# All steps of a fused window-attention and two-layer kernel in a new order, with q and k of batch 0 loaded ahead of most of V

## The chip, the cores and the metric

The kernel runs on one core of one Trainium2 chip. The metric is the device time of that core in microseconds (us). The kernel before takes 312.04 us, the median of three runs from 312.03 to 312.27.

## What is computed

The reference is attention over a causal window of 64 positions, then two matrix products with `h - tanh(h)` between them.

```python
batch, n_heads, seq, head_dim = (8, 8, 576, 64)
...
scores = scale * np.matmul(q, k.transpose(0, 1, 3, 2))
mask = (rel >= 0) & (rel < window)          # rel = query position - key position
attn = softmax(np.where(mask, scores, -1e9))
x = (attn @ v), heads side by side           # 4608 x 512
h = x @ w_in                                 # 512 x 2048
g = h - np.tanh(h)
return g @ w_out                             # 2048 x 512
```

All inputs and the output are float32; the kernel works in bfloat16 and sums in float32.

## The kernel before

**Tiling.** The sequence of a batch is cut into nine windows of 64 queries; a window needs the 128 keys that end with it. Heads are worked in pairs: pair g of 32 holds heads g % 4 and g % 4 + 4 of batch g // 4. Attention writes its result transposed into chunks of 512 tokens (`x_chunk`); a chunk is the moving operand of the first layer, 16 blocks of 128 hidden columns with four matmuls of 512 columns each, and its `g` is the stationary operand of the second layer, four blocks of 128 tokens with 16 matmuls each. There are nine chunks; chunk 0 needs all of batch 0 but its last window.

**The order is written out by hand.** The kernel turns the framework's scheduling off and plays `PLAN`, a string of 1146 words. A word is a step with its arguments, for instance `Rp.1.0.4`: step Rp, pair 1, group 0, PSUM bank 4. A last letter p, a, v or s names the engine: GpSimd (POOL), ScalarE (ACT), VectorE (DVE), SyncE (SP). Each engine works off its own steps in the order of the words; between engines the framework puts semaphore waits wherever two steps touch the same place. So the place of a word decides what stands behind it on the same engine, and which of two steps that touch one place comes first.

The steps that the text speaks of:

- `lk.g`, `lq.g` (`load`, L92 to L109): k or q of pair g from DRAM. On GpSimd's queue the transfer also converts to bfloat16; on SP's it does not. `LV.b.i` (`load_rows`, L140 to L144): 128 rows of V of batch b for all heads (64 rows for i = 4), into the tile `vw`, 64 values a head with a 65th column beside them. `lv.b.pair.half` (`load_v`) and `lt.b`: V of batch 1, head by head. `wi.i`, `wo.i`: blocks of the weights. All but two of the loads are issued by GpSimd, and its queue takes a further one only when the eighth before it has landed.
- `mv.i` (`pads_v`, L199 to L201): two memsets on VectorE in `vw`, the 65th column to one (L200) and a first block of zeros (L201). `mt`, `mq`: zeros beside k and in q. `i`, `h`, `n`: an identity and two masks, made on GpSimd.
- `Z.b` (`cross_rows`, L146 to L150): two copies on VectorE that put the rows of V that a window shares with its neighbour on the other half of the partitions. For batch 1 these are `za` and `zb`, a pair at a time.
- `U.n` (`warm_up`, L217 to L220): n matmuls of 512 columns on a tile of zeros, whose result nobody reads.
- `ck.g`, `cq.g` (`cast`): reorders k or q in SBUF. `Fp.g`, `Ep.g` (`tr`): transposes on TensorE. `Fc`, `Ec`, `Ea`, `Eb` (`put`): copies of these into `kT`, `qp` or `qT`, of which there are two each, used by even and odd pairs.
- `Rp` (`scores`, L273 to L293), `Rx` (`probs`, the exponentials on ScalarE), `M` (`masking`), `N` (`put_mask`).
- `P.g` (`pv`, L334 to L342), `PP.g` (`pv_pairs`): the product with V; its 65th column gives the sum of each row. `D.g`, `DS.g`, `DH.g.n`, `DR`, `DN`: division by that sum, on VectorE.
- `Xp`, `Xc` (L399 to L415): transposes of the result and copies into the chunk.
- `H.c.m` (`first_layer`, matmuls at L437), `A.c.m` (tanh, L445), `G.c.m` (h - tanh(h), L451), `W.c.s.part` (second layer, L480 and L473), `O.c.s` (copy and store of the output).

TensorE's queue goes without a branch through transposes, scores, products with V and both layers, so any one of them that waits holds all the rest. PSUM has eight banks, addressed by number in the words.

```python
    def load_rows(b, i):
        w, n = vw[b % 2], min(128, S - 128 * i)
        nc.gpsimd.dma_start(out=w[:, 2 * i + 1, :, 0:D] if i < NF else w[64:128, 2 * i, :, 0:D],
                            in_=v[b, :, 128 * i:128 * i + n].rearrange("h p d -> p h d"))
...
    def pads_v(i):
        nc.vector.memset(vw[i][:, :, :, D], 1.0)
        nc.vector.memset(vw[i][0:64, 0], 0.0)
```

Of the kernel before, what the change touches and what calls it, by code (L numbers as in the profile page):

```python
# [15 lines left out]
def kernel(  # L16
# [491 lines left out]
    def subtract(c, m, s=None):
# [14 lines left out]
        H=first_layer, A=tanh, G=subtract, W=yp_mm, O=y_out)  # L523

    def play(script):
# [14 lines left out]
        lq.8.p H.0.2 A.0.1 G.0.0 n lv.1.3.1 Rp.4.2.4 ck.7.v G.0.1 H.0.3 Rx.4.2.4 Rp.5.2.4 wo.0 A.0.3 Rx.5.2.4  # L540
        G.0.3 Fp.7.3 H.0.4 Rp.4.0.4 A.0.2 N G.0.2 H.0.6 Rx.4.0.4 Fc.7.3.a M.5 A.0.4 za.1.0.v G.0.4 H.0.5 A.0.6
        lv.1.3.0 Fp.6.3 Rp.4.1.4 A.0.5 Fc.6.3.a G.0.5 H.0.7 zb.1.0.p Ep.7.3 A.0.7 G.0.6 H.0.8 Ea.7.3.a G.0.7
        cq.6.v A.0.8 H.0.9 Eb.7.3.v G.0.8 za.1.1.p Rx.4.1.4 H.0.10 A.0.9 zb.1.1.p lt.1 M.4 Rp.7.0.4 Ep.6.3
        A.0.10 H.0.11 Eb.6.3.a Rx.7.0.4 G.0.9 wo.2 G.0.10 H.0.12 A.0.11 lq.9.p wo.1 Rp.7.2.4 Rx.7.2.4 H.0.13
        wo.3 Ea.6.3.v G.0.11 A.0.12 cq.8.v lk.9.p Rp.6.1.4 H.0.14 G.0.12 Rx.6.1.4 Ep.8.3 ck.8.v H.0.15 A.0.14
# [95 lines left out]
```

## Time and profile before

| | |
|---|---|
| median of three runs | 312.04 us |
| the profiled execution, its own time | 311.42 us |
| its span, from the first instruction to the last | 309.7 us |
| mean granted TensorE clock | 0.989 of full speed |
| busy: TensorE (PE), VectorE, ScalarE, GpSimd | 301.3, 183.7, 156.2, 103.0 us |
| first matmul of the first layer, H.0.0 | starts at 27.93 us |
| last matmul ends | 306.52 us |
| matmuls of the first layer (L437) and of the second (L480) | 380 ns each in the rows, 216 ns from start to start |
| dummy matmuls (L220) | 27 |

A busy time is a union over an engine's instructions, and matmuls overlap, so their rows last longer than the distance of their starts. "PEclk" is the clock that the chip granted to TensorE. L143 and the like are lines of the kernel file.

### The profile page before, as it was taken

Reading aid. Unit: us, or ns where it says so; the run is one execution under the profiler, and the core shown is the slowest. Engines: PE = TensorE matmul, PEld = TensorE weight load, DVE = VectorE, ACT = ScalarE, POOL = GpSimd, SP = SyncE. Lnnn points to the kernel's source line nnn. Section 1 sums busy time; section 2 is a strip of 40 time slices with the busy share of each in tenths; the row PEclk is TensorE's granted clock in tenths of the full one; section 3 lists DMA queues with packets and bytes.
Section 4 is the critical chain, followed back from the end, with each engine's and each line's share of the span. In section 5 each row is a group of like instructions: output and inputs, shape, how many; then the busy total and the mean of one; then the engine's idle time right before and its main releaser. Section 6 shows DMA issues by size and latency. Waiting matters only on the chain.

```text
span 309.7 us, 6275 instructions
## 1 busy us (share of the span) xinstructions
PE 301.3 (97%) x2522; PEld 159.8 (52%) x2522; DVE 183.7 (59%) x321; ACT 156.2 (50%) x266; POOL 103.0 (33%) x139
## 2 busy tenths in 40 slices
PE   8798999999999999999999999999999999999995
PEld 3456555556555545555555555555554444444443
DVE  3558796758947757767557585836566433353301
ACT  3556878579527644643725445555253333444300
POOL 8996475695195028203942700000000000000000
PEclk9959999999999999999999999999999999999999
DMA  9999999999999969998999998350015000000012
GB/s 151 132 176 199 197 182 187 181 169 141 145 137 162 148 117 151 164 155 125 159 160 177 161 179 117 89 134 35 3 70 110 34 35 34 34 34 36 37 65 102
DMA packets 133436, 37.33 MB, mean 121 GB/s; under 512 B 122016, under 2 KB 127904, under 8 KB 133408
## 3 DMA queue, kind: packets, MB, share of 16 engines
q0 software_dynamic: 91184, 18.06, 75.3%
q1 hardware_dynamic: 42224, 18.88, 31.3%
q8 instruction: 19, 0.31, 0.4%
q14 instruction: 9, 0.07, 0.1%
HBM read 36.70 MB, written 9.44 MB: 149 GB/s over the span
## 4 chain that ended last, share of the span: by engine, by line
PE 89%; DVE 3%; POOL 3%; DMA 2%; issue 1%; ACT 1%; POOLq 0%; ACTq 0%; DVEq 0%
PE ps L480 39%; PE ps L437 38%; PE ps L354 3%; PE ps L310 2%; DMA qall<-in_q_dram 2%; POOL vw L143 1%; PE ps L253 1%; DVE gT L451 1%; PE ps L473 1%; PE ps L292 1%; PE ps L403 1%; DVE qt L90 1%; PE ps L281 1%; POOL kall L108 1%; ACT th L445 1%
## 5 line engine op out<-in xcount | busy, mean ns | idle before, releaser
L451 DVE TENSOR_TENSOR gT<-ps,th 128x512 bf16<-128x512 f32 x144 | 97.7, 687 | 79.6 <-ACT th L445 79.0
L437 PE MATMUL ps<-xT,wi 128*128 128x512 bf16 x576 | 140.4, 380 | 0.5 <-DVE gT L451 0.2
L445 ACT ACTIVATE th<-ps 128x512 f32<-128x512 f32 x144 | 85.2, 598 | 100.0 <-PE ps L437 98.6
L480 PE MATMUL ps<-w_out_sb,gT 128*128 128x512 bf16 x560 | 134.3, 380 | 0.0
L437 PEld LDWEIGHTS <-wi 128*128 128x128 bf16 x576 | 63.0, 114 | 54.7 <-issue 0.9
L480 PEld LDWEIGHTS <-gT 128*128 128x128 bf16 x560 | 53.7, 98 | 60.9
L143 POOL DMA_DIRECT2D vw<-in_v_dram x35 | 30.5, 882 | 16.6 <-DVE q L90 9.0
L159 POOL DMA_DIRECT2D kall<-in_k_dram x25 | 21.6, 877 | 26.0 <-DMA kw<-kall 24.9
L159 POOL DMA_DIRECT2D qall<-in_q_dram x25 | 21.8, 879 | 20.9 <-DMA qw<-qall 17.5
L320 ACT ACTIVATE pt<-ps 128x1024 bf16<-128x1024 f32 (+1 forms) x30 | 23.3, 812 | 6.1 <-PE ps L310 5.9
L88 ACT ACTIVATE ysb<-ps 128x512 f32<-128x512 f32 (+1 forms) x20 | 11.6, 582 | 24.8 <-PE ps L480 19.7
L90 DVE COPY ysb<-ps 128x512 f32<-128x512 f32 (+1 forms) x17 | 11.6, 680 | 20.2 <-PE ps L480 19.5
L329 DVE TENSOR_TENSOR pt<-pt,ps 128x1152 bf16<-128x1152 bf16 x28 | 20.5, 746 | 3.2 <-ACT pt L320 2.8
L324 ACT ACTIVATE pt<-ps 128x384 bf16<-128x384 f32 (+2 forms) x32 | 16.9, 528 | 5.3 <-PE ps L292 3.4
L374 DVE TENSOR_TENSOR xs<-ps,rcp 128x384 bf16<-128x384 f32 x28 | 14.8, 550 | 0.2
L354 PEld LDWEIGHTS <-pt 128*64 128x64 bf16 x504 | 9.1, 111 | 5.1 <-issue 1.6
L354 PE MATMUL ps<-vw,pt 128*64 128x65 bf16 x504 | 10.7, 197 | 0.0
L220 PE MATMUL ps<-warm 128*128 128x512 bf16 x27 | 9.2, 498 | 1.1 <-DVE warm L197 1.1
L88 ACT ACTIVATE kt<-ps 128x576 bf16<-128x576 bf16 x10 | 6.5, 648 | 6.5 <-PE ps L253 3.5
L108 POOL DMA_DIRECT2D kall<-in_k_dram x11 | 7.3, 668 | 3.2 <-DMA wi<-in_moe_w_in_dram 1.8
L130 POOL DMA_DIRECT2D vw<-in_v_dram x8 | 6.7, 843 | 4.6 <-DMA wi<-in_moe_w_in_dram 4.5
L292 PE MATMUL ps<-qt,kt 128*128 128x128 bf16 x72 | 8.0, 219 | 0.0
(76 smaller groups left out, 160.5 us busy)
## 6 DMA issues: line engine op xcount, KB each, us to landing
out_dram<-ysb SPq DMA_DIRECT2D x35, 256.0 KB, 3.5
vw<-in_v_dram POOLq DMA_DIRECT2D x28, 128.0 KB, 8.6
kall<-in_k_dram POOLq DMA_DIRECT2D x20, 128.0 KB, 7.1
qall<-in_q_dram POOLq DMA_DIRECT2D x20, 128.0 KB, 7.0
w_out_sb<-in_moe_w_out_dram POOLq DMA_DIRECT2D x4, 512.0 KB, 10.1
kall<-in_k_dram POOLq DMA_DIRECT2D x11, 144.0 KB, 5.2
qall<-in_q_dram POOLq DMA_DIRECT2D x11, 144.0 KB, 7.2
vw<-in_v_dram POOLq DMA_DIRECT2D x16, 64.0 KB, 7.0
```

What stands on the lines that cost most here:

```text
L88: nc.scalar.activation(o, i, ACT.Copy)
L143: nc.gpsimd.dma_start(out=w[:, 2 * i + 1, :, 0:D] if i < NF else w[64:128, 2 * i, :, 0:D], in_=v[b, :, 128 * i:128 * i + n].rearrange("h p ...
L159: nc.gpsimd.dma_start(out=token_rows(b, n)[0:c, i], in_=(q if n == "q" else k)[b, :, 128 * i:128 * i + c].rearrange("h p d -> p h d"))
L320: nc.scalar.activation(o, sp, ACT.Exp, scale=scale)
L324: nc.scalar.activation(PT[g % NPT][:, js[0]:js[0] + len(js), :].rearrange("p i (h t) -> p i h t", h=2), sp, ACT.Exp, scale=scale)
L329: nc.vector.tensor_tensor(p, p, mask.unsqueeze(1).to_broadcast([128, 2 * NJ, 64]), ALU.mult)
L354: nc.tensor.matmul(ps[r, bank, 65 * i:65 * i + 65], PT[(g + r2) % NPT][:, j, r], vw[b % 2][:, j, p0 + r2 + NP * h, :], start=True, stop=True)
L374: nc.vector.tensor_tensor(xs[b % 2][:, 0:6, p0 + n // 2, :], ov[:, :, 0:D], sums[g][:, n].to_broadcast([128, 6, D]), ALU.mult)
L437: nc.tensor.matmul(hp, w_in_tile(ki, m), chunk_tile(c)[:, n.start // 64:n.stop // 64, ki % 2, 64 * (ki // 2):64 * (ki // 2) + 64], start=( ...
L445: nc.scalar.activation(th[:, n], hp, ACT.Tanh)
L451: nc.vector.tensor_tensor(gT[c][:, m, columns(s)], hp, th, ALU.subtract)
L480: nc.tensor.matmul(yp, gT[c][:, m, s * 128:(s + 1) * 128], w_out_sb[:, m, :], start=n == 1 and i == 0, stop=n == 4 and i == 3)
```

## The change

Two things change. A function `first_layer_part` is added, with a step Hp for it, which no word of the list uses. And the list is replaced: the same 1146 words but for the order, for the engine of some of the copies, and for the banks of many transposes and scores, which lay in bank 2, 3 or 4 and now lie in banks 0 to 7. The numbers of transfers, matmuls and dummy matmuls are the same. Here is the start of both lists, up to the first layer, and the new function; the rest of the list is in a new order as well.

```diff
         hidden[c, m, s] = hp_mm(c, m, s)
 
+    def first_layer_part(c, m, half):
+        n = turn("h", c, m)
+        hp = ps[:, m % 2 if c > 1 else (m + c) % 3, :]
+        for i in range(2):
+            nc.tensor.matmul(hp, w_in_tile(half + 2 * i, m), chunk_tile(c)[:, :, half, 64 * i:64 * i + 64],
+                             start=n == 1 and i == 0, stop=n == 2 and i == 1)
+        hidden[c, m, None] = hp
+
     def tanh(c, m, s=None):
         hidden[c, m, s] = squash(s, hidden[c, m, s])
 
...
@@ PLAN
-        mt.1 mt.0 lk.1.p lq.1.p i u mv.0 LV.0.0 lk.5.p U.1 lk.0.s U.1 lq.0.s lq.3.p U.4 LV.0.3 LV.0.4 h LV.0.1
-        cq.0.a U.13 mq.0 mv.1 U.1.3 ck.1.a cq.1.v mq.1 Fp.1.2 Ep.1.3 LV.0.2 Fc.1.2.a U.2 ck.0.v Fp.0.2 lk.3.p
-        Ec.1.3.v Fc.0.2.v Rp.1.1.4 Ep.0.3 Ec.0.3.v Rx.1.1.4 lq.2.p Rp.1.0.0 lv.1.1.1 lk.2.p lq.5.p Rx.1.0.0 U.4
-        Rp.0.1.4 Rp.0.0.0 ck.5.a lk.4.p Z.0 Rx.0.1.4 Ep.3.3 Rx.0.0.0 Fp.3.2 lv.1.0.0 lk.6.p lq.4.p P.0 Fc.3.2.a
-        Ec.3.3.v lk.7.p D.0 Ep.2.3 Rp.3.1.4 Ec.2.3.a Rp.3.0.0 U.1.2 Rx.3.1.4 Fp.5.3 wi.0 Fp.2.2 cq.5.a Fc.5.3.v
-        P.1 lv.1.1.0 ck.4.v D.1 Rx.3.0.0 Fc.2.2.a Ep.5.3 Rp.2.1.4 Eb.5.3.a lq.7.p lv.1.0.1 wi.1 Rp.2.0.0
-        Rx.2.1.4 P.3 Rx.2.0.0 Ea.5.3.v wi.2 Fp.4.3 lq.6.p P.2 Xp.0.0.1.2 cq.4.v Fc.4.3.a Rp.5.0.4 D.3 DS.2
-        Xp.0.0.0.3 Rx.5.0.4 DH.2.0 Xc.0.0.1.2.a Xc.0.0.0.3.v DH.2.1 Xp.0.1.0.3 Xc.0.1.0.3.a Xp.0.1.1.2 Rp.5.1.4
-        Ep.4.3 Xc.0.1.1.2.v ck.6.v Ea.4.3.v Eb.4.3.v H.0.0 H.0.1 lv.1.2.0 A.0.0 Rx.5.1.4 lk.8.p cq.7.v lv.1.2.1
...
+        lq.0.s lk.0.s u LV.0.2 i lk.1.p ck.1.v cq.0.v mt.1 lq.1.p lq.3.p lk.3.p U.1 U.13 ck.0.a LV.0.3 U.4
+        Fp.0.0 U.4 Fc.0.0.a lq.2.p cq.1.v Fp.1.2 Ep.1.7 U.2 LV.0.0 mt.0 LV.0.1 Fc.1.2.v h Fp.3.6 Ep.3.3 Ec.1.7.a
+        lk.5.p lk.2.p Ep.0.5 LV.0.4 Rp.1.1.4 Rp.1.0.0 lq.5.p Rx.1.1.4 Ec.0.5.a Rx.1.0.0 mv.0 Ec.3.3.v lq.4.p
+        mv.1 Rp.0.1.4 U.1 Ep.2.2 Rp.0.0.0 Rx.0.1.4 Z.0 mq.0 Fc.3.6.a Rx.0.0.0 Rp.3.1.4 Fp.2.3 Rx.3.1.4 Rp.3.0.0
+        cq.5.v Fc.2.3.a lv.1.1.1 Ec.2.2.a P.0 lk.4.p lq.6.p Ep.5.3 Rp.2.1.4 U.1.2 D.0 Rx.3.0.0 wi.0 Rp.2.0.0
+        Rx.2.1.4 P.1 cq.4.v lv.1.1.0 Ep.4.2 mq.1 D.1 Rx.2.0.0 P.2 P.3 DS.2 lq.7.p ck.4.v DH.2.0 D.3 Ea.4.2.a
+        Eb.5.3.a Ea.5.3.a Fp.4.4 Xp.0.0.0.0 Xp.0.0.1.7 n lk.6.p U.1.3 DH.2.1 Xp.0.1.0.3 Xc.0.0.1.7.v Fc.4.4.a
+        wi.1 Eb.4.2.a Rp.4.0.4 Xp.0.1.1.5 ck.5.v Xc.0.1.1.5.v cq.6.v Rp.4.1.6 Xc.0.0.0.0.a Rp.4.2.7 Fp.5.1
+        Xc.0.1.0.3.a Fc.5.1.v H.0.0 Rx.4.0.4 A.0.0 Rx.4.2.7 cq.7.v ck.6.v Ep.6.4 H.0.1 H.0.2 G.0.0 A.0.1
+        Ea.6.4.v A.0.2 Rx.4.1.6 H.0.3 Rp.5.1.7 Rx.5.1.7 A.0.3 G.0.1 lk.7.p Rp.5.2.3 za.1.1.p wi.2 lq.8.p G.0.2
+        Ep.7.6 Rp.5.0.5 lv.1.0.1 Rx.5.2.3 H.0.5 ck.7.v Eb.7.6.v Fp.6.7 N lk.8.p A.0.5 Fp.7.3 G.0.3 H.0.4
+        Ea.7.6.a Rx.5.0.5 Fc.7.3.a H.0.6 Eb.6.4.v wo.2 A.0.4 Fc.6.7.v Rp.6.1.5 Rp.7.2.3 Rp.6.0.6 G.0.5 Rp.7.0.4
+        G.0.4 Rp.7.1.7 H.0.8 A.0.6 lv.1.0.0 lt.1 H.0.7 A.0.8 wo.1 A.0.7 G.0.6 M.4 G.0.8 zb.1.1.p wo.0 Rx.6.1.5
...
```

On GpSimd the loads went lk.1, lq.1, LV.0.0, lk.5, lq.3, LV.0.3, LV.0.4, LV.0.1, LV.0.2, lk.3, lq.2 and so on; they now go LV.0.2, lk.1, lq.1, lq.3, lk.3, LV.0.3, lq.2, LV.0.0, LV.0.1, lk.5, lk.2, LV.0.4, lq.5, lq.4, lv.1.1.1, lk.4, lq.6, wi.0. On SP lk.0 and lq.0 change places. On VectorE mv.0 and mv.1 stood ahead of the first V load of their tile; mv.0 now stands behind the five loads of batch 0, after Fc.1.2 and ahead of Ec.3.3, mv.1 and Z.0, and mv.1 still ahead of lv.1.1.1. On TensorE the transposes and scores of pair 3 and the transposes of pair 2 now come ahead of P.0; they came behind it, but for the transposes of pair 3.

More of the change, by code (lines that the diff above doesn't have):

```diff
@@ L522 @@
         P=pv, D=norm, DS=norm_sums, DH=norm_half, PP=pv_pairs, DR=recip_pairs, DN=norm_pairs, Xp=x_tr, Xc=x_put, Y=x_dma,
-        H=first_layer, A=tanh, G=subtract, W=yp_mm, O=y_out)
+        H=first_layer, Hp=first_layer_part, A=tanh, G=subtract, W=yp_mm, O=y_out)
     def play(script):
@@ L541 @@
[L541 to L545, printed above, removed]
@@ new lines @@
+        G.0.14 DR.4 lv.1.2.1 G.0.15 W.0.0.2 Rp.8.2.3 W.0.0.1 DN.4.2 DN.4.0 lk.9.p Rp.8.1.7 lq.10.p M.7 lk.10.p
+        Rx.8.2.3 W.0.1.1 DN.4.1 W.0.1.2 W.0.0.0 Xp.1.0.0.3 Rp.8.0.4 lr.3.4 lq.11.p G.0.13 Rx.8.1.7 Xp.1.0.1.5
+        LV.2.3 M.6 W.0.1.0 W.0.1.3 cq.9.v lk.11.p W.0.0.3 O.0.1.a W.0.3.1 zb.1.2.v Ep.9.1 O.0.0.a W.0.3.2
+        W.0.3.0 zb.1.3.p za.1.2.v za.1.3.v Xc.1.0.0.3.v Rx.8.0.4 Xc.1.0.1.5.a LV.2.0 PP.6 ck.9.a cq.10.v M.8
+        Ep.10.3 DR.6 LV.2.2 W.0.2.3 W.0.2.2 Ea.10.3.a ck.10.a Eb.9.1.a Ea.9.1.a DN.6.1 Eb.10.3.a LV.2.1 Fp.9.6
@@ new lines @@
+        W.0.2.0 DN.6.2 DN.6.0 Fc.9.6.v Xp.1.1.1.1 W.0.2.1 Xp.1.1.0.3 lr.3.2 Rp.9.1.7 O.0.2.a cq.11.v
+        Xc.1.1.0.3.v Xc.1.1.1.1.v W.0.3.3 Rp.9.2.5 H.1.0 Rx.9.1.7 ck.11.a Rx.9.2.5 LV.2.4 qr.3.0 qr.4.3 A.1.0
+        Ep.11.6 Rp.9.0.4 Eb.11.6.a Fp.11.5 Rx.9.0.4 qr.4.4 Fp.10.3 H.1.1 O.0.3.v qr.3.4 H.1.2 Fc.11.5.a LV.3.3
+        LV.3.1 A.1.1 Fc.10.3.a G.1.0 A.1.2 H.1.3 A.1.3 Z.2 G.1.1 Rp.10.2.7 Rp.10.0.4 H.1.4 Rx.10.2.7 A.1.4 G.1.2
+        G.1.3 Ea.11.6.a H.1.5 M.9 G.1.4 H.1.6 A.1.5 Rx.10.0.4 A.1.6 H.1.7 G.1.5 A.1.7 PP.8 lr.4.4 lr.3.0 lr.3.3
@@ new lines @@
+        H.1.8 G.1.6 Rp.11.2.4 A.1.8 G.1.7 Rp.11.0.3 H.1.10 A.1.10 DR.8 H.1.9 LV.3.4 DN.8.0 lr.3.1 qr.3.3 DN.8.2
+        G.1.8 DN.8.1 qr.3.2 Rp.11.1.5 H.1.11 Rx.11.2.4 Rx.11.0.3 Rp.10.1.4 A.1.9 A.1.11 Rx.11.1.5 LV.3.2 mk
+        G.1.10 G.1.9 tq.3.4 H.1.13 tk.3.2 Rx.10.1.4 tq.3.0 A.1.13 tk.3.0 tq.4.4 tk.3.4 tq.3.3 Xp.2.0.1.3 G.1.11
+        H.1.12 H.1.14 Xp.2.0.0.4 A.1.12 M.10 M.11 PP.10 G.1.13 G.1.12 tz.3.a Xc.2.0.0.4.a DR.10 A.1.14 W.1.0.0
+        H.1.15 Xc.2.0.1.3.a DN.10.2 mz tk.3.1 DN.10.1 DN.10.0 tk.3.3 W.1.0.1 W.1.0.2 Xp.2.1.1.6 A.1.15
@@ new lines @@
+        W.2.1.1 tk.5.2 G.3.0 M.17 A.3.1 H.3.2 A.3.2 tq.5.2 W.2.1.3 tk.5.4 tq.5.1 M.16 G.3.1 PP.16 H.3.3 G.3.2
+        lr.6.4 O.2.1.v A.3.3 H.3.4 lr.5.1 LV.5.4 A.3.4 DR.16 DN.16.2 G.3.3 DN.16.1 G.3.4 tk.5.0 LV.5.3 qr.6.4
+        tk.5.1 tq.5.0 W.2.2.0 tk.5.3 tq.5.3 H.3.5 W.2.2.1 LV.5.1 LV.5.2 A.3.5 DN.16.0 H.3.6 A.3.6 S.18 G.3.5
+        H.3.7 Sx.18.0 A.3.7 Sx.18.2 G.3.6 H.3.8 W.2.2.2 M.18 G.3.7 Sx.18.1 W.2.2.3 A.3.8 G.3.8 H.3.9 A.3.9
+        H.3.10 M.19 PP.18 G.3.9 A.3.10 O.2.2.v H.3.11 DR.18 W.2.3.3 G.3.10 A.3.11 H.3.12 lr.7.3 A.3.12 DN.18.0
@@ new lines @@
+        O.3.1.v A.4.4 S.22 G.4.5 H.4.7 G.4.4 H.4.6 W.3.2.2 Sx.22.0 A.4.7 W.3.2.0 W.3.2.3 G.4.7 Sx.22.1 A.4.6
+        G.4.6 Sx.22.2 M.22 M.23 H.4.9 A.4.9 W.3.2.1 PP.22 G.4.9 O.3.2.v tk.6.1 H.4.8 H.4.11 W.3.3.1 A.4.8 G.4.8
+        DR.22 DN.22.2 A.4.11 W.3.3.2 H.4.10 tq.6.1 tq.6.2 A.4.10 G.4.11 H.4.13 G.4.10 A.4.13 G.4.13 DN.22.1
+        DN.22.0 W.3.3.3 H.4.12 H.4.15 tq.6.4 A.4.12 G.4.12 W.3.3.0 Y.5 O.3.3.a A.4.15 H.4.14 A.4.14 tz.6.a
+        W.4.0.0 W.4.0.2 S.24 G.4.15 G.4.14 Z.6 H.5.0 W.4.0.3 H.5.1 A.5.0 W.4.0.1 Sx.24.1 G.5.0 A.5.1 O.4.0.a
@@ new lines @@
+        G.5.1 Sx.24.0 Sx.24.2 M.25 H.5.2 M.24 qr.7.2 qr.7.1 qr.7.3 A.5.2 LV.7.0 G.5.2 W.4.1.0 W.4.1.1 H.5.3
+        PP.24 A.5.3 H.5.4 A.5.4 G.5.3 DR.24 DN.24.0 DN.24.2 W.4.1.2 lr.7.0 tk.7.3 tk.7.0 H.5.5 A.5.5 G.5.4
+        LV.7.2 qr.7.0 W.4.1.3 G.5.5 DN.24.1 tk.7.4 H.5.6 S.26 A.5.6 O.4.1.a H.5.7 lr.7.2 W.4.2.0 G.5.6 H.5.8
+        A.5.7 qr.7.4 tq.7.3 tq.7.0 tk.7.2 tq.7.2 G.5.7 H.5.9 W.4.2.1 tq.7.1 A.5.9 Sx.26.0 W.4.2.3 W.4.2.2 LV.7.1
+        A.5.8 G.5.9 G.5.8 lr.7.1 H.5.11 Sx.26.1 Sx.26.2 M.27 LV.7.3 H.5.10 LV.7.4 O.4.2.a W.4.3.2 M.26 PP.26
@@ L611 @@
+        A.8.8 A.8.9 G.8.8 G.8.9 W.7.2.1 W.7.2.3 O.7.2.v H.8.10 H.8.11 W.7.3.0 A.8.11 G.8.11 W.7.3.2 H.8.15
+        A.8.10 G.8.10 H.8.12 A.8.15 W.7.3.3 W.7.3.1 A.8.12 G.8.12 H.8.14 G.8.15 O.7.3.a H.8.13 W.8.1.2 A.8.14
+        A.8.13 G.8.14 G.8.13 W.8.0.0 W.8.0.1 W.8.0.3 W.8.1.0 W.8.0.2 O.8.0.v W.8.1.1 W.8.1.3 W.8.2.3 W.8.2.1
+        W.8.3.2 W.8.2.2 W.8.2.0 O.8.1.v W.8.3.3 W.8.3.1 O.8.2.v O.9.0.a W.8.3.0 O.8.3.a"""
     play(PLAN)
```

99 lines of the change are left out of this document (33 added, 66 removed).

## The prediction

> **What bounds the kernel now.** I read the page first: engines, then slices.
>
> ```profile
> PE 301.3 (97%) x2522; PEld 159.8 (52%) x2522; DVE 183.7 (59%) x321; ACT 156.2 (50%) x266; POOL 103.0 (33%) x139
> ...
> PE   8798999999999999999999999999999999999995
> ...
> PEclk9959999999999999999999999999999999999999
> ```
>
> TensorE is busy 97% of the span, and only the first four slices (7.74 us each) are short of 9; the third has a granted clock of about one half. To see how much is left I asked for the busy time by stage (columns: stretch, its length, then busy us and count for PE, PEld, DVE, ACT, POOL, the granted clock, the DMA share, GB/s).
>
> ```profile
> 13.10:16.50 3.40, 1.07 (x42) 0.80 (x36) 1.93 (x3) 1.22 (x2) 3.40 (x6) 1.00 1.41 174
> 16.50:19.90 3.40, 2.92 (x40) 1.42 (x36) 1.26 (x3) 1.89 (x4) 2.89 (x5) 0.50 1.43 179
> 19.90:23.30 3.40, 3.40 (x56) 2.55 (x55) 2.22 (x5) 2.04 (x5) 3.40 (x6) 0.50 1.18 173
> ...
> 45.00:306.50 261.50, 261.50 (x2094) 136.71 (x2092) 154.01 (x262) 127.53 (x217) 68.69 (x83) 1.00 1.04 112
> ```
>
> From 45 us on TensorE never idles, at full clock. The products are the same after the change, so 261.5 us and the 3.2 us behind the last product stay; there the new order can only add a wait. What can be won lies ahead of the first first-layer product, H.0.0, which starts at 27.93 us (timeline), and in about 1.2 us of small gaps between 28 and 51 us (starts of successive matmuls against their usual distance, 0.40 at 40.8 the largest). The chain of waits says what sets the start:
>
> ```profile
> 7.76 0.94 POOL hide L226
> ...
> 9.55 0.90 POOL vw L143
> 10.45 0.61 POOL kall L108
> 11.05 5.96 DMA qall<-in_q_dram
> ```
>
> GpSimd issues one load after another; what it issues last, TensorE gets last. The loads' own rows:
>
> ```profile
> L143 POOL DMA_DIRECT2D vw<-in_v_dram x5: 721/902/940, 3.3 to 9.5; - x5
> ...
> DMA to landing us min/median/max: 4.7/5.0/6.5
> ```
>
> A V load costs GpSimd 0.90 us (the 64-row one 0.72), a q or k load 0.66, and lands 5.0 us after issue. VectorE's crossing copies wait for the last V load:
>
> ```profile
> 14.52 0.70 DVE L149 COPY vw<-vw 64x2080 bf16<-64x2080 bf16 x1 [3.37 <-DMA vw<-in_v_dram]
> 15.23 0.79 DVE L150 COPY vw<-vw 64x2080 bf16<-64x2080 bf16 x1
> ```
>
> So P.0, the first product with V, starts at 16.08.
>
> **The change, part by part.** All times count from the span's start.
>
> *The V loads end later.* The new GpSimd order is LV.0.2, i, lk.1, lq.1, lq.3, lk.3, LV.0.3, lq.2, LV.0.0, LV.0.1, h, lk.5, lk.2, LV.0.4. GpSimd's first load starts at 1.37. Ahead of LV.0.4 lie three more V loads at 0.90 and one at 0.92 (3.62), seven q/k loads at 0.66 (4.62), i (2.77 to 3.37, 0.60) and h with its gaps (7.11 to 8.65, 1.54): 1.37 + 3.62 + 4.62 + 0.60 + 1.54 = 11.75. It lands at 16.8 (16.4 to 18.3 by the ends 4.7 and 6.5). In the kernel before the last V load, LV.0.2, was issued at 9.55 and landed at 14.50.
>
> *A wait that the new order adds.* mv.0 (L200, L201) ran before any V load; now it stands behind all five. L200 writes the column of ones between the columns that the loads fill. In the trace the first V load, issued at 3.32, carries a wait on the counter that VectorE raises, and ahead of it VectorE had written that tile only by mv.0; of the two memsets L200 raises the counter, L201 does not. So the program treats L200 and a V load as touching the same place, and I take it that with the order turned round L200 waits for all five loads. This wait is not in the trace: at the low end it costs nothing (the loads are then waited for by Z.0 alone), at the high end everything queued behind it. I take the high end, because the same pair of instructions is ordered in this trace. Queued behind mv.0 on VectorE are Ec.3.3, mv.1, Z.0; for Ec.3.3 waits Rp.3.1.4 on TensorE, and for mv.1 waits lv.1.1.1 on GpSimd, with every later load behind it.
>
> *To P.0.* 16.8 + mv.0 0.78 (1.30 to 2.08) + Ec.3.3 0.76 + mv.1 0.77 (2.90 to 3.67) + Z.0 1.50 (14.52 to 16.02) + 0.1 of gaps = 20.7, against 16.02 before.
>
> *From P.0 to H.0.0.* In the kernel before this took 27.93 - 16.08 = 11.85 us, with q and k of pair 2 still to come (Ep.2.3 at 17.06) and TensorE at half clock to 23.3. Now the transposes and scores of pair 3 and the transposes of pair 2 are done, and VectorE's queue sets the pace: mq.0 0.54, cq.5 0.35, three norms D at 1.04 (0.22 + 0.82), cq.4 0.35, mq.1 0.54, DS.2 0.21, ck.4 0.35, DH.2 0.49 + 0.42, Xc 0.42 + 0.22, ck.5 0.35, Xc 0.42 = 7.78. To this come some 0.6 of waits: D.1 for P.1, which waits for D.0, and D.3 for P.3. ck.4 needs lk.4: mv.1 ends at 19.2, then lv.1.1.1 0.8 and lk.4, issued at 20.0, landing at 25.0, when VectorE gets there. ACT's last Xc fits (done by 28.8). wi.0, issued at 21.4, has 7.45 from issue to landing in the trace: 28.8. H.0.0 then starts at 20.7 + 7.8 + 0.6 = **29.1**, 1.2 later than 27.93. By then TensorE has done one group of three scores more (three of pair 4 instead of two of pair 5): 3 x 0.056 = 0.17. Net **+1.0 us**.
>
> *The clock.* Rp.0.0.0 ends at about 14.9 and Rp.3.1.4 waits for Ec.3.3 to 18.4: 3.5 us without a product. The dummies (27 before and after) are all queued elsewhere. In the kernel before, 1.07 us busy in 3.4 were followed by 6.8 us at a clock of 0.50; so this is likely again. At 0.50 a pair of score groups took 1.5 us (22.23 to 23.89, less waits) against 1.1 (9.39 to 10.8, less waits), and Ep 0.66 against 0.42; between 20.7 and 24 that puts P.1, and with it D.1, about 0.8 later. At the low end, no throttling, nothing; I take **+0.5**.
> The Trainium skill ("TensorE: Matmul & The Clock Gate", "Why this matters for your kernels") warns of idle gaps over some 3 us between bursts of matmuls; the trace shows the half clock behind a stretch that was one third busy. By that rule the change, which is to fill the first waits, goes cold as the old one did, and the sum would have +0.8 in place of +0.5.
>
> *The first layer of chunk 0.* GpSimd has nothing to issue from 13.7 (lq.4) to 19.2, so no load lands between about 18.5 and 24. Later za.1.1 on GpSimd waits for lv.1.1.0 (29.6), so wi.2 is issued at 30.3 and lands, behind lk.7 (34.0) with its 5.0 us of transfer (29.62 to 34.62 before), at 39.0. H.0.8 would start at 38.6: 0.4 of wait. With 0.3 for VectorE's queue ahead of it that is 0.7, in place of the 1.2 of gaps before: **-0.5**. wo.0 to wo.3 land at 43.6 to 52.4 and are wanted from 48 to 54.7, V of batch 1 by 47.6: just in time. If each load takes as long as wi.0 did (3.77 behind its forerunner instead of 2.5), this is +2.0 instead.
>
> *The rest*: transfers are the same in number and size, and later loads have tens of us to spare (lq.11 landed at 52.6 before). Other banks for transposes and scores change where a product waits for a copy; the trace has no row for that: from -0.3 to +1.0 over 12 pairs, and I take 0, nearest to the 45 to 306 us stretch. SP's queue has the same two loads, swapped; both are used after 4.96, when both have landed. The new function has no step in the list: 0. The end has the same last products and copies: 0.
>
> Sum: 1.0 + 0.5 - 0.5 = **+1.0 us**. The profiled execution took 311.42 us (span 309.7 and 1.7 around it); it lies 0.6 below the median of 312.04, and I put the shift on the median: **313.0**.
>
> **Rivals.**
> 1. *mv.0 does not wait* (faster). Then Z.0 starts at 16.8 and ends at 18.3, Ec.3.3 is early, GpSimd is never held; H.0.0 at 18.3 + 7.8 + 0.3 = 26.4, 1.7 less with the extra scores, and another 0.5 as weights come earlier: 309.8. For it: the two regions share no element. Against it: the wait in the trace. Chance 0.17.
> 2. *Loads land sooner* (faster). The load of k on SP's queue landed 3.1 us after issue. If the V loads did so with the shorter queue ahead of them, LV.0.4 would be there at 14.9, H.0.0 at 14.9 + 3.9 + 7.8 + 0.6 = 27.2, 0.9 less with the extra scores, and GpSimd held less: 311.1. Against it: 4.7 to 6.5 in the rows above, none under 4.3 in the first 23 us on GpSimd's queue. Chance 0.03. The Trainium skill ("DMA: Bandwidth & Descriptors", "Anatomy of one DMA — SWDGE (gpsimd) path") fits about 2.0 us plus bytes over 436 GB/s per transfer, an estimate of 2.3 for 128 KB, by which H.0.0 would come at 26.4; the trace has 5.0 and disagrees.
> 3. *The hole in the loads starves the first layer* (slower). The place is wi.1 and wi.2; it decides once wi.2 lands after 39. With 3.77 per weight block and lk.7 behind it, wi.2 lands at 41.5: 2.0 in place of -0.5, so 1.0 + 0.5 + 2.0 and VectorE's copies bunching behind: 315.6. For it: GpSimd waited 4.5 us for a wi landing already. Chance 0.18.
> 4. *No change that counts*: the later V is just made up by the warm clock and the gaps: 312.0. Chance 0.12.
>
> **The numbers.** Forecast 313.0, chance 0.50, own range 311.9 to 314.6. A measurement of this kernel tells apart some 0.2%, 0.6 us. Faster: rivals 1 and 2 and 0.03 of the forecast, 0.23. Same: rival 4 and 0.06 of the forecast, 0.18. Slower: 0.59. The range runs from 309.9, inside rival 1, to 315.6.
>
> **What would show it.** The chain should go through L200 of vw, waiting for a V load near 16.8, then L149 near 19.2; TensorE idle for about 3.5 us before it, the clock near 0.5 behind it; GpSimd idle from 13.7 to 19.2; H.0.0 near 29.1. A memset at L200 that starts at about 10 us makes the first step wrong and rival 1 right. TensorE idle over 1 us between 30 and 42 at L437, released by wi, makes rival 3 right. Idle time beyond 60 us would be a wait I have not seen.

## The result, and the profile after

The changed kernel takes **320.47 us**, the median of four runs from 319.94 to 320.84; beside it the kernel before took 312.03 (311.12 to 312.27). The ratio is 1.0275, 95% interval 1.0248 to 1.0301: slower by 2.7%, and outside the range of the prediction (309.9 to 315.6). The profiled execution took 320.69 us, its span is 318.9, 9.2 more than before. The page of the changed kernel, engines and slices (7.97 us each):

```profile
PE 304.5 (95%) x2522; PEld 161.3 (51%) x2522; DVE 181.7 (57%) x319; ACT 154.1 (48%) x268; POOL 102.8 (32%) x139
...
PE   8759999999999999999999689999999999999996
...
PEclk9966999999999999999999969999999999999999
```

PE is the busy share of TensorE in tenths, PEclk the clock that it was granted. The start is there as foretold, with slices of 7 and 5 and a low clock behind them. But slices 23 and 24 (a 6 and an 8, with a clock of 6 tenths in the second) lie at 175 to 191 us, where the kernel before showed nines. The busy time by stage says it in microseconds (stretch, its length, PE busy, PEld, DVE, ACT, POOL, granted clock, DMA share, GB/s):

```profile
45.00:176.00 131.00, 131.00 (x1215) 70.56 (x1214) 90.15 (x161) 73.71 (x131) 73.91 (x89) 1.00 1.98 159
176.00:192.00 16.00, 12.16 (x78) 5.64 (x77) 5.15 (x8) 5.62 (x10) 1.57 (x2) 0.79 1.46 127
```

From 45 us on TensorE misses nothing outside these 16 us (123.77 of 123.80 us behind them), as before. And the waits of TensorE, longest first:

```profile
PE ps L286 <- DVE qp L90: 3.3, 1, 3.3
PE ps L305 <- ACT q L88: 2.6, 1, 2.6
PE ps L437 <- DMA xT<-xs: 1.3, 1, 1.3
```

The first is Rp.3.1.4 at the start, waiting for Ec.3.3. The second (S.24, scores of batch 6) and the third (H.5.0, first layer of chunk 5) are new and were not in the prediction.

Each step H has four first-layer matmuls in the trace, in the order of the list, and their starts place the loss. H.0.0 starts at 30.96 us (27.93 before), H.2.0 is 2.81 us later than before and H.3.0 2.77; the last matmul ends at 315.77, 9.25 later than 306.52. So about 2.8 us come from the start and **6.4 us from the stretch around 180 us**. The first figure is that of one execution: in the four profiled experiments below that have the same words up to there, H.2.0 is 2.5 to 4.1 us later than before.

### The start

VectorE's timeline in the changed kernel:

```profile
17.13 0.12 DVE L200 MEMSET vw<- 128x72 bf16 x1 [7.39 <-DMA qall<-in_q_dram]
...
17.84 0.69 DVE L90 COPY qp<-ps 128x576 bf16<-128x576 bf16 x1
18.73 0.12 DVE L200 MEMSET vw<- 128x72 bf16 x1 [0.21 <-issue]
...
19.52 0.90 DVE L149 COPY vw<-vw 64x2080 bf16<-64x2080 bf16 x1
```

VectorE idles for 7.39 us ahead of mv.0. The view names a load of q, but that load only shares its counter with LV.0.3. The waiting itself stands in the rows of L200 on VectorE's sequencer (ns: shortest, median, longest):

```profile
L200 DVEq EVENT_SEMAPHORE  x2: 21/1752/3484, 11.4 to 13.3; - x2
```

The second wait runs from 13.3 us for 3.48, to 16.8, where LV.0.4 lands (16.77); the experiments confirm that the order of memsets and V loads is the cause. Behind mv.0 come Ec.3.3, mv.1 and Z.0, as in the prediction.

### The stall at 177 to 189 us

Two transfers on SP's queue are late. SP's rows (L496 is the store of O.3.2, L164 is tk.6.1, L172 are tq.6.1, tq.6.2 and tq.6.4, L422 is Y.5):

```profile
169.23 0.33 SPq L496 DMA_DIRECT2D out_dram<-ysb  x1
169.65 1.21 SPq L164 DMA_TRANSPOSE kw<-kall  x1
170.96 4.24 SPq L172 DMA_TRANSPOSE qw<-qall  x3
176.42 7.52 SPq L422 DMA_TRANSPOSE xT<-xs  x2
```

One is tq.6.4, the last transposing transfer for S.24, which stands behind that store: issued at 173.74, it lands at 182.22. The other is the first of the two transfers of Y.5, which brings the first three windows of batch 5 into chunk 5: issued at 176.42, landed at 185.28; H.5.0 starts at 185.33. Y.5 waits for the divisions DN.22 on VectorE. These are VectorE's lines, first in the kernel before, then in the changed one (L362 is DR.22, L374 and L371 are DN.22, L451 is a step G):

```profile
167.84 0.27 DVE L362 RECIPROCAL rcp<-ps 128x18 f32<-128x18 f32 x1
168.15 0.56 DVE L374 TENSOR_TENSOR xs<-ps,rcp 128x384 bf16<-128x384 f32 x1
168.62 0.68 DVE L451 TENSOR_TENSOR gT<-ps,th 128x512 bf16<-128x512 f32 x1
169.22 0.55 DVE L374 TENSOR_TENSOR xs<-ps,rcp 128x384 bf16<-128x384 f32 x1
169.68 0.55 DVE L371 TENSOR_TENSOR xs<-ps,rcp 128x384 bf16<-128x384 f32 x1
```

```profile
171.07 0.26 DVE L362 RECIPROCAL rcp<-ps 128x18 f32<-128x18 f32 x1
171.36 0.56 DVE L374 TENSOR_TENSOR xs<-ps,rcp 128x384 bf16<-128x384 f32 x1
171.84 0.68 DVE L451 TENSOR_TENSOR gT<-ps,th 128x512 bf16<-128x512 f32 x1
173.91 0.69 DVE L451 TENSOR_TENSOR gT<-ps,th 128x512 bf16<-128x512 f32 x1 [1.39 <-ACT th L445]
174.77 0.69 DVE L451 TENSOR_TENSOR gT<-ps,th 128x512 bf16<-128x512 f32 x1 [0.17 <-ACT th L445]
175.38 0.55 DVE L371 TENSOR_TENSOR xs<-ps,rcp 128x384 bf16<-128x384 f32 x1
175.85 0.55 DVE L374 TENSOR_TENSOR xs<-ps,rcp 128x384 bf16<-128x384 f32 x1
```

From DR.22 to the end of the divisions it was 2.4 us before and is 5.3 now: the list has G.4.11, G.4.10 and G.4.13 between DN.22.2 and the other two, and these wait for tanh, which waits for TensorE. The list leaves TensorE work until about 181 us (where H.5.0 starts in an experiment below that has neither wait); a transfer of 8.86 us that leaves at 176.42 is too late for it.

### The profile page after: what moved, and what is told of

Its sections match the earlier page's. It is cut to its first block, busy times and chain, and to the rows that moved or that the text cites. A ratio compares the mean times of both kernels' runs of the same rounds, so it can differ in the third digit from the quotient of the medians.

```text
span 318.9 us, 6262 instructions
## 1 busy us (share of the span) xinstructions
PE 304.5 (95%) x2522; PEld 161.3 (51%) x2522; DVE 181.7 (57%) x319; ACT 154.1 (48%) x268; POOL 102.8 (32%) x139
## 3 DMA queue, kind: packets, MB, share of 16 engines
HBM read 36.70 MB, written 9.44 MB: 145 GB/s over the span
## 4 chain that ended last, share of the span: by engine, by line
PE 83%; DMA 10%; POOL 4%; issue 1%; DVE 0%; ACT 0%; POOLq 0%; DVEq 0%
PE ps L480 38%; PE ps L437 38%; PE ps L354 3%; DMA wi<-in_moe_w_in_dram 3%; DMA xT<-xs 3%; DMA vw<-in_v_dram 3%; PE ps L310 2%; DMA qall<-in_q_dram 1%; POOL vw L143 1%; PE ps L473 1%; POOL kall L108 1%; POOL qall L108 1%; PE ps L292 1%; PE ps L403 1%; PE ps L253 1%
## 5 line engine op out<-in xcount | busy, mean ns | idle before, releaser
L451 DVE TENSOR_TENSOR gT<-ps,th 128x512 bf16<-128x512 f32 x144 | 97.0, 686 | 89.4 <-ACT th L445 88.7
L437 PE MATMUL ps<-xT,wi 128*128 128x512 bf16 x576 | 140.7, 382 | 1.6 <-DMA xT<-xs 1.3
L437 PEld LDWEIGHTS <-wi 128*128 128x128 bf16 x576 | 63.5, 114 | 57.7 <-issue 1.6
L88 ACT ACTIVATE ysb<-ps 128x512 f32<-128x512 f32 (+2 forms) x23 | 13.4, 581 | 33.4 <-PE ps L480 20.6
L329 DVE TENSOR_TENSOR pt<-pt,ps 128x1152 bf16<-128x1152 bf16 x28 | 20.4, 750 | 8.7 <-ACT pt L320 5.3
L159 POOL DMA_DIRECT2D qall<-in_q_dram x25 | 21.5, 876 | 3.4 <-DMA vw<-in_v_dram 1.7
L90 DVE COPY ysb<-ps 128x512 f32<-128x512 f32 x14 | 9.6, 687 | 11.4 <-PE ps L480 11.3
L374 DVE TENSOR_TENSOR xs<-ps,rcp 128x384 bf16<-128x384 f32 x28 | 14.6, 550 | 0.2
L88 ACT ACTIVATE qt<-ps 64x576 bf16<-64x576 bf16 x13 | 8.4, 642 | 2.4 <-issue 1.6
L108 POOL DMA_DIRECT2D qall<-in_q_dram x11 | 7.2, 656 | 1.9 <-PE ps L292 1.2
```

The source lines that it names most:

```text
L88: nc.scalar.activation(o, i, ACT.Copy)
L108: eng.dma_start(out=t, in_=(q if n == "q" else k)[b, pr::NP].rearrange("h (p e) d -> p h (e d)", e=E))
L159: nc.gpsimd.dma_start(out=token_rows(b, n)[0:c, i], in_=(q if n == "q" else k)[b, :, 128 * i:128 * i + c].rearrange("h p d -> p h d"))
L329: nc.vector.tensor_tensor(p, p, mask.unsqueeze(1).to_broadcast([128, 2 * NJ, 64]), ALU.mult)
L437: nc.tensor.matmul(hp, w_in_tile(ki, m), chunk_tile(c)[:, n.start // 64:n.stop // 64, ki % 2, 64 * (ki // 2):64 * (ki // 2) + 64], start=( ...
L451: nc.vector.tensor_tensor(gT[c][:, m, columns(s)], hp, th, ALU.subtract)
```

## The experiments

Two theories were set against each other at first. **A**: the losses at the start and at 180 us are separate, each made by the order of a few words. **B**: the second is a consequence of the first, since everything runs later. The times beside which they stand are those of the kernel before on the same chip (medians of 311.5 to 311.7 us, and 312.03 beside the changed kernel, so that times of different experiments compare to some 0.5 us).

### Halves of the two lists

```diff
 PLAN: words of after up to H.1.0
-PLAN: remaining words in the order of after
+PLAN: remaining words in the order of before
```

> The list of after up to H.1.0 (the start, all of chunk 0), then the remaining words in the order of before. Theory A (the two losses are separate: the start costs 2.9 us by the start of H.0.0, 30.96 against 27.93 less 0.17 of scores done earlier, and the stall at 177 to 189 us costs about 6.2 us and belongs to the order around O.3.2 and the copies tk and tq of batch 6): about 315 us, no stall at 177 to 189 us. Theory B (the rest of the new order would be as good as the old; the stall comes because everything, the loads too, runs late after the late start): about 320 us, a stall near 180 us stays.

Measured: 315.59 us (315.13 to 316.06), ratio 1.011 (1.0066 to 1.0154), and no stall at 177 to 189 us. H.0.0 started at 29.81 in this execution, 1.9 behind before; with a wait of 1.0 for wi that ends at 39.75 us and one of 1.6 for a step G that ends at 71.15, where the halves meet, it is 3.6 behind at H.2.0 and stays so to the end. This is as A has it.

```diff
 PLAN: words of before up to H.1.0
-PLAN: remaining words in the order of before
+PLAN: remaining words in the order of after
```

> The list of before up to H.1.0, then the remaining words in the order of after. Theory A: the stall at 177 to 189 us is there without the new start; about 318 us (312.0 + 6.2). Theory B: no stall, about 312 us.

Measured: 321.72 us (320.88 to 322.55), ratio 1.0306 (1.0265 to 1.0347). The stall is there with the old start: S.24 waits 3.3 us and H.5.0 0.8. B falls. The 318 of A was too low because where the halves meet 2.6 us more go by 76 us (the largest part, 1.3 us, in waiting for exponentials): a price of the splice, which the change itself does not pay (its lag shrinks from 3.0 at H.0.0 to 2.8 at H.2.0).

### The memsets early

```diff
-u LV.0.2
+u mv.0 mv.1 LV.0.2
...
-Rx.1.0.0 mv.0 Ec.3.3.v lq.4.p mv.1 Rp.0.1.4
+Rx.1.0.0 Ec.3.3.v lq.4.p Rp.0.1.4
```

> After, but mv.0 and mv.1 (the memsets of the 65th column and of the block of zeros) stand ahead of LV.0.2, the first load of V, as they stood ahead of the loads in before. Theory A: the memset at L200 no longer waits for the landing of the last V load (16.77 us); what P.0 waits for is then Z.0 after that landing and the exponentials, so that Rp.3.1.4 is no longer held to 18.6 us by the copy Ec.3.3 behind the memsets; P.0 near 19.0 in place of 21.19 and H.0.0 at 27 to 29 in place of 30.96; 317 to 318.5 us in all, the stall at 177 us unchanged. Rival (the loads of V, not the place of the memsets, set the start: Z.0 needs LV.0.4 anyway): H.0.0 within 0.5 us of 30.96, and 320 to 321 us.

Measured: 316.45 us (315.23 to 317.11), ratio 1.0133 (1.009 to 1.0176), 4.0 less than the changed kernel. H.0.0 starts at **24.74**, earlier than expected and 3.2 earlier than in the kernel before. VectorE in this kernel:

```profile
13.39 0.76 DVE L90 COPY qp<-ps 128x576 bf16<-128x576 bf16 x1 [3.92 <-PE ps L286]
14.20 0.70 DVE L149 COPY vw<-vw 64x2080 bf16<-64x2080 bf16 x1
```

Ec.3.3 runs at 13.39 and no longer at 17.84, and Z.0 at 14.20, 0.02 behind the landing of LV.0.1 and well ahead of that of LV.0.4 (16.64): Z.0 copies whole blocks of 128 rows to the other half and does not touch the last, short one. Only P.0 needs LV.0.4, and starts at 17.1 (21.19 in the changed kernel). The rival falls. Of the 5.6 us that H.4.0 is ahead of the changed kernel, 4.55 are left at the end: the stall near 175 us grows by one, as tq.6.4 lands only 4.75 us sooner.

### The four transfers ahead of a store

```diff
-O.3.1.v
+O.3.1.v tk.6.1 tq.6.1 tq.6.2 tq.6.4
...
-O.3.2.v tk.6.1
+O.3.2.v
...
-H.4.10 tq.6.1 tq.6.2 A.4.10
+H.4.10 A.4.10
...
-H.4.15 tq.6.4 A.4.12
+H.4.15 A.4.12
```

> After, but tk.6.1, tq.6.1, tq.6.2 and tq.6.4 (four transfers on SP's queue) stand right behind O.3.1.v, ahead of the store O.3.2.v, behind which SP held them to 169.65 us and later. Theory A (SP's order: the transfers stood behind a store that waits for VectorE's copy at 168.5 us): they are issued at 163 to 168 us and land by 173 us, S.24 no longer waits 2.6 us, Y.5 is issued as before or earlier, and the clock stays up; 3 to 6 us are gained, 314.5 to 317.5 us. Rival (the DMA engines are full with GpSimd's loads for batch 7 at 168.9 to 177.4 us): the transfers still land at 177 us or later or Y.5's first transfer does, a stall of 3 us or more stays, and the gain is under 2 us.

Measured: 320.82 us (319.57 to 321.63). No gain, as by the rival. Of the two waits one is gone: the four were issued at 162.8 to 168.0 and landed at 170.8 to 174.9, and S.24 no longer waits. H.5.0 does instead:

```profile
PE ps L437 <- DMA xT<-xs: 4.4, 1, 4.4
```

Y.5 was issued at 176.57, as before the edit, though SP's queue ahead of it was empty, and took 8.8 us to land. So its late issue has a cause of its own, which the rival did not name; its long way is what the rival said, and is tried further down. The two waits stand one behind the other: what S.24 does not wait, H.5.0 does.

### The divisions early, alone and with the transfers

```diff
-DN.22.2 A.4.11 W.3.3.2
+DN.22.2 DN.22.1 DN.22.0 A.4.11 W.3.3.2
...
-G.4.13 DN.22.1 DN.22.0 W.3.3.3
+G.4.13 W.3.3.3
```

> After, but DN.22.1 and DN.22.0 stand right behind DN.22.2, ahead of the steps G.4.11, G.4.10 and G.4.13 behind which VectorE held them to 175.38 and 176.39 us. Nothing else is moved. Theory C (two transfers are late side by side: tq.6.4 for S.24, held on SP behind O.3.2, and Y.5 for H.5.0, held by DN.22.0 on VectorE; mending one leaves the other): Y.5 is issued at 175.2 us at the earliest, since it still stands behind tq.6.4 on SP; S.24 still waits 2.6 us or more, H.5.0 then waits 0 to 1.3 us; 319 to 320.5 us. Rival D (the late normalization alone makes the stall): 315 to 317 us.

Measured: 320.87 us, ratio 1.025 (1.0174 to 1.0326); its four executions spread from 316.5 to 321.8. The interval reaches down to 317, so that the time alone does not exclude rival D. The profiled execution, the longest at 321.79, speaks for C: S.24 still waits 2.9 us, Y.5 was issued at 176.64, behind tq.6.4 (175.19) on SP, and H.5.0 does not wait. It had lost 1.7 us by H.4.15 (it waits 1.5 for wi near the start, the changed kernel 0.3), and from there to the last matmul it takes 1.9 less than the changed kernel; so the edit by itself may be worth up to 1.9 us, which the total hides. That one execution of four was 4 us shorter stays unexplained, as it has no profile.

```diff
-O.3.1.v
+O.3.1.v tk.6.1 tq.6.1 tq.6.2 tq.6.4
...
-DN.22.2 A.4.11 W.3.3.2
+DN.22.2 DN.22.1 DN.22.0 Y.5 A.4.11 W.3.3.2
...
```

> Both edits: tk.6.1, tq.6.1, tq.6.2 and tq.6.4 right behind O.3.1.v, and DN.22.1, DN.22.0 and then Y.5 right behind DN.22.2. Theory C: Y.5 is issued at 172.5 to 173.5 us, lands at about 182 us, neither S.24 nor H.5.0 waits over 1 us, the clock stays full, and 5 to 6.5 us of the 320.5 us go: 314 to 315.5 us. Rival E (the DMA engines can't bring these transfers any sooner while GpSimd's loads for batch 7 run): H.5.0 still waits 2 us or more and the time is over 317 us.

Measured: **314.77 us** (314.39 to 316.55), ratio 1.0112 (1.0077 to 1.0148), 5.7 less than the changed kernel. The chain of waits in this kernel:

```profile
172.03 0.47 DVE xs L374
172.50 0.03 DVE gT L451
172.53 8.43 DMA xT<-xs
180.96 0.05 issue
181.01 1.05 PE ps L437 x4
```

Y.5 leaves 3.9 us earlier and lands just as TensorE arrives. Up to H.4.15 this kernel runs 0.07 us behind the changed one; H.5.0 is 4.3 earlier, H.5.8 6.3, and so is the end. So the stall cost 4.3 us up to H.5.0, 3.9 of them waits, and 1.9 of half clock behind it. C holds, E falls.

### Without the loads beside them

```diff
-LV.7.0
...
-lr.7.0
...
-LV.7.2 qr.7.0
...
-lr.7.2
...
-qr.7.4
...
-LV.7.1
...
-lr.7.1
...
-LV.7.3
...
-LV.7.4
```

> After without the ten loads that GpSimd issues from 168.88 to 177.37 us (LV.7.0 to LV.7.4, lr.7.0, lr.7.1, lr.7.2, qr.7.0, qr.7.4): batch 7 is then computed from what lies in the buffers, batch 5's data in part. Theory C: the order on SP and VectorE stays, so Y.5 is still issued at 176.4 us; without the loads beside it, it lands in 5 to 6 us (5.90 us in before with three loads ahead of it) in place of 8.86, and the tq in 5 to 6 us in place of 8.5 to 9; S.24's and H.5.0's waits shrink to 0 to 1.5 us together: 315 to 317 us. Rival F (8 us is what such a transposing transfer takes whatever runs beside it): the waits stay, 320 to 321 us.

This kernel leaves out the ten loads of batch 7 that GpSimd issues from 168.88 to 177.37 us. Measured: 314.11 us (313.11 to 315.79), ratio 1.009 (1.0063 to 1.0117), a little below the 315 to 317 expected. The transfers tq of the changed kernel, then of this one (issue times; ns a transfer keeps SP; time to landing):

```profile
L172 SPq DMA_TRANSPOSE qw<-qall x3: 1288/1353/1457, 171.0 to 173.7; - x3
DMA to landing us min/median/max: 8.5/8.6/9.0
```

```profile
L172 SPq DMA_TRANSPOSE qw<-qall x3: 1217/1217/2568, 172.5 to 175.1; - x3
DMA to landing us min/median/max: 2.6/3.7/4.4
```

Issued no earlier, they land in 2.6 to 4.4 us in place of 8.5 to 9.0; Y.5's first, issued at 178.00, lands in 2.73 in place of 8.86. S.24 and H.5.0 both start without a wait; the one wait of 1.5 us at L437 in this execution ends at 153.24, ahead of the first layer of chunk 4, before the loads that were left out. From H.4.15 to the last matmul it takes 133.6 us, 140.1 in the changed kernel and 133.8 in the one with both edits. Rival F falls: most of the price of such a transfer is the company that it has. The changed kernel shows the same by itself: the four transfers of Y.6 and Y.7, from 214 us on, when GpSimd loads nothing, land in 2.3 to 4.3 us. The Trainium skill ("DMA: Bandwidth & Descriptors", "Queues, rings and completion order") says that each DMA engine takes the queues that have work in turn, a packet at a time. The trace agrees in direction: SP's transfers take two to three times as long (8.6 us against 3.7, 8.86 against 2.73) while GpSimd's queue has eight loads in flight. The turns themselves are shown by no run here.

### More dummies in the wait

```diff
-Rx.0.0.0 Rp.3.1.4
+Rx.0.0.0 U.14 Rp.3.1.4
```

> After with 14 more dummy matmuls ahead of Rp.3.1.4, in the wait from 14.9 to 18.6 us. It isolates the price of the low clock, 0.5 of full speed from 18.65 to 28.89 us in after. Theory: the clock stays full to H.0.0, the waits for V stay, and H.0.0 starts 1.5 to 2.5 us earlier counted from the landing of LV.0.4 (14.2 us behind it in after); 318 to 319 us. Rival (the clock falls for other reasons, or the work between P.0 and H.0.0 waits for VectorE and ScalarE and not for TensorE): under 0.7 us, 320 to 321 us.

Measured: 319.61 us (317.71 to 322.45), which this spread can't tell from 320.47; the profile can. Stages of the changed kernel, then of this one (columns as above):

```profile
15.00:18.60 3.60, 0.31 (x4) 0.12 (x5) 1.22 (x3) 0.73 (x2) 0.00 (x0) 1.00 0.43 57
...
22.00:28.90 6.90, 6.63 (x108) 4.92 (x109) 4.79 (x12) 3.58 (x6) 4.31 (x9) 0.50 1.11 148
```

```profile
15.00:18.60 3.60, 3.28 (x35) 1.74 (x33) 1.67 (x5) 0.44 (x1) 0.20 (x1) 1.00 0.27 41
...
22.00:28.50 6.50, 5.78 (x129) 4.30 (x127) 5.77 (x17) 5.63 (x10) 3.57 (x8) 1.00 1.14 152
```

The clock stays full. From P.0 to H.0.0 it is 8.1 us (20.4 to 28.5) in place of 9.8 (21.19 to 30.96): the low clock cost **1.7 us** there, as the theory had it. (The five other profiled executions with the same words up to H.0.0 and a half clock took 9.3 to 9.6 us, which makes it 1.3 to 1.5.) Two thirds of the 2.5 us by which H.0.0 is earlier are lost again in chunk 0, where H.0.0 to H.0.8 takes 11.1 us in place of 9.5: TensorE waits 0.9 us for a cast of k and 0.6 for a copy, both on VectorE. So in the total the low clock weighs less than 1.7 us, and how much less is not settled.

### All edits, and the better of both lists

The edits of the third and of the sixth experiment together, in the changed kernel:

```diff
-u LV.0.2
+u mv.0 mv.1 LV.0.2
...
-O.3.1.v
+O.3.1.v tk.6.1 tq.6.1 tq.6.2 tq.6.4
...
-DN.22.2 A.4.11 W.3.3.2
+DN.22.2 DN.22.1 DN.22.0 Y.5 A.4.11 W.3.3.2
...
```

> After with all three edits: mv.0 and mv.1 ahead of LV.0.2; tk.6.1, tq.6.1, tq.6.2 and tq.6.4 right behind O.3.1.v; DN.22.1, DN.22.0 and Y.5 right behind DN.22.2. If the two losses are separate and additive (4.0 us by the early memsets, 5.7 us by the other two): 310 to 311.5 us. If the early start only meets the transfers of batch 6 sooner (with the early memsets alone the stall at 172 to 185 us was 7 us, not 6.2): 312 to 314 us.

Measured: **310.02 us** (308.7 to 310.25), ratio to before **0.9932** (0.9917 to 0.9948), shorter than both kernels. 320.47 - 4.0 - 5.7 = 310.8: additive, the rival falls. Its page:

```profile
PE 299.4 (98%) x2522; PEld 158.5 (52%) x2522; DVE 182.0 (59%) x319; ACT 153.8 (50%) x268; POOL 102.3 (33%) x139
...
PE   8799999999999999999999999999999999999995
```

The same start with the early memsets, up to H.3.0, and from there the words in the order of before:

```diff
 PLAN: words of after up to H.3.0
-u LV.0.2
+u mv.0 mv.1 LV.0.2
...
-PLAN: remaining words in the order of after
+PLAN: remaining words in the order of before
```

> The list of after up to H.3.0 with mv.0 and mv.1 ahead of LV.0.2, then the remaining words in the order of before. In the run with the early memsets alone H.0.0 stood at 24.74 us (27.93 in before) and H.3.0 2.83 us ahead of before; from there the old order lost nothing in the first splice. Theory (the new start without its wait is better than the old one, and the old rest has no stall): 308 to 309.5 us, faster than both kernels. Rival (the 3 us of lead are eaten by loads that come no sooner, as in the old order at 64 to 75 us): 310.5 to 312 us.

Measured: 309.18 us (308.69 to 310.69), ratio 0.9913 (0.9898 to 0.9927). The rival falls. The profiled execution was the longest, 310.69, with a wait of 2.4 us at L437 for wi.2, which landed at 36.70. In the next kernel za.1.1.p, a copy on GpSimd, was moved behind that load:

```diff
-za.1.1.p wi.2
+wi.2
...
-lv.1.0.0
+za.1.1.p lv.1.0.0
```

> As the one before last, but the copy za.1.1.p on GpSimd stands ahead of lv.1.0.0 and no longer ahead of wi.2; it waits for a load of V of batch 1 (24.4 us) and so held wi.2 from 20.2 to 25.02 us. Theory: wi.2 is issued at 21 to 22 us and lands by 32 us, the first layer of chunk 0 no longer waits for it (1.1 us of steps over 0.3 us near 32.6 and 34.2 us), and 0.5 to 1 us are gained over that kernel. Rival: the landings are spread by the DMA engines, and nothing changes within 0.4 us.

Measured: **308.27 us** (307.87 to 309.11), ratio 0.9886 (0.9871 to 0.9902), the fastest of all. GpSimd's timeline, with za and then without it ahead of wi.2:

```profile
24.89 0.76 POOL L180 DMA_DIRECT2D wi<-in_moe_w_in_dram  x1
```

```profile
20.85 0.77 POOL L180 DMA_DIRECT2D wi<-in_moe_w_in_dram  x1
```

Issued 4.0 us earlier, it landed only 2.3 earlier (34.37, not by 32), and 0.4 us of wait remain. The gain of 0.9 us has the size expected, the landing has not; the executions of the two kernels overlap (308.69 to 310.69 and 307.87 to 309.11), so that the gain is likely and not sure.

> As the one before, with three more dummy matmuls ahead of Fp.3.6 and two ahead of Ep.0.5, in waits of 0.8 and 0.6 us near 8.9 and 10.3 us, behind which the clock fell to 0.5 of full speed from about 11.5 to 15 us. Theory: the clock stays full and H.0.0 starts 0.5 to 1.5 us earlier; the time gains 0 to 1 us, since wi.0 (landing at 23.6 us) and the loads behind it come no sooner. Rival: the dummies delay the transposes by their 0.2 us each and nothing is gained.

```diff
-Fp.3.6
+U.3 Fp.3.6
...
-Ep.0.5
+U.2 Ep.0.5
```

Measured: 309.70 us (five executions from 307.99 to 309.96 and one of 313.81): no gain. The premise had gone: the mean clock of the kernel without them was 0.999 already.

## Why the prediction was wrong

**Right, by its own steps.** LV.0.4 issued at 11.75 and landed at 16.8: 11.15 and 16.77. mv.0 waits for all V loads: yes, at 17.13, and the edit that puts it ahead of them takes the wait away. From the landing of LV.0.4 to P.0 it was 3.9 by the sum and 4.4 in each of the seven profiled executions with this order. Rp.3.1.4 to 18.4: 18.57. GpSimd without work from 13.7 to 19.2: from 13.1 to 19.15. P.0 at 20.7: 21.19. wi.2 issued at 30.3 and landing at 39.0: 30.85 and 40.39. Rival 2 (loads sooner) did not come: 5.3 to 6.6 us. Rival 3 did not either: TensorE waited 0.3 us for wi.

**The step that failed** is "The rest", 0 us, with the sentence that "later loads have tens of us to spare". It looked at the loads from DRAM and left out the transposing transfers on SP's queue and what they wait for. These have no slack of tens of us: in the kernel before, the last one for S.24 landed at 171.36, 3.3 us ahead of it (174.62), and Y.5 was issued at 169.79 and its first transfer landed at 175.69, 3.2 us ahead of the first layer of chunk 5 (H.5.1 at 178.89); the new order issues it 6.6 us later, with eight loads of GpSimd in flight beside it. The cost of the stall, from the two edits that remove it, is 5.7 us by the medians and 6.3 by the traces. The two lists showed the places: one step G between the divisions DN.22 before and three after, a store ahead of four transfers. So the step put at 0 measured some 6.4 of the 9.2 us by which the span grew. The prediction said that idle time beyond 60 us would be a wait that it had not seen; that is what it was. The other banks, for which it took 0 as well, are no large cost: with the three edits the new list, banks and all, takes 310.02 us.

**The clock** was a term of the right kind and too small: 0.5 us taken, 1.7 measured by the dummies for P.0 to H.0.0. The half clock lasted from 18.65 to 28.89 us, 10.24 us and not the 6.8 of the kernel before, so that it covered most of the way to the first layer and not just P.1. The Trainium skill ("TensorE: Matmul & The Clock Gate", "Terms") puts the penalty at the throttled time times the missing share of the clock, an estimate of 5.1 us for the whole stretch and of 3.9 for the 7.7 us of it behind P.0. The two traces have 1.7 there. With the clock full, VectorE is busy 5.77 of the last 6.50 us ahead of H.0.0, as much as TensorE; that it sets part of the pace is likely, and no run shows it apart.

**The first layer of chunk 0** was put at -0.5; H.0.0 to H.0.15 took 17.09 us against 16.69, +0.4: the gaps did not go, and wi.2 came 1.4 us later than foretold. In the five other executions with the same words this took 16.7 to 18.4 us, so that the term is not known to better than 1 us. P.0 was 0.5 later than the 20.7 of the sum. The start as a whole is +2.8 where 1.0 + 0.5 - 0.5 was summed.

**Rival 1 did not come, and was underpriced.** In the changed kernel mv.0 waits. With mv.0 free of its wait the rival gave H.0.0 at 26.4; the edit measured 24.74. It let Z.0 wait for LV.0.4, which Z.0 does not read.

One reading was loose and cost nothing: of the first four slices before, the third is a 9 (only its clock is low), and the last slice is a 5.

So the new start, of which q and k ahead of V is the main part, is good for 3.2 us at H.0.0 (what each of its moves is worth was not tried); a pair of memsets put behind the loads took 6.2 away there, and the order around batch 6 another 6.3 further on.

## What to carry to other kernels

When a list of steps is put in a new order, do not cost the steady part at nothing because it was full before: for each transfer take the instruction that releases it, what is queued ahead of that one on its own engine, and the work that is left between there and the use, and hold this against the landing time under the loads that run at the same time (here 8.5 to 9.0 us, not the 2.6 of a quiet queue). Put first writes of a buffer, however small, ahead of the loads that fill it. Two waits one behind the other hide each other: an edit that removes one and gains nothing has not shown that it was harmless.

## What the runs showed of the hardware

The half clock comes in stretches of a length: 10.24 us at the start, 6.83 us (182.49 to 189.31) behind the stall, 6.8 in the kernel before, that is three, two and two times 3.41 us, and 3.4 behind the stall in two of the experiments (the divisions early, the dummies). The Trainium skill ("TensorE: Matmul & The Clock Gate", "What's actually happening") states a window of 3.41 us that runs freely. The lengths agree; and in six profiled executions with the same words up to P.0 the half clock began 0.0 to 2.3 us behind the landing of the last V load, and lasted 10.24 us in five of them and 6.83 in one, so that it does not hang on the work alone. A wait of 3.3 us with 0.31 us of work in 3.6 was enough to bring it on.

A transposing transfer on SP's queue took 2.6 to 4.4 us to land without the ten loads of batch 7 (2.3 to 4.3 for Y.6 and Y.7 in the changed kernel). Beside them it took 7.2 to 9.0, and 12.2 for Y.5's second one. Its issue keeps SP 1.2 to 1.5 us in 51 of the 60 of the changed kernel, and longer in the rest, up to 6.2 us for Y.5's second one.
